# The score layout of the last segment and the order of the second half, in a fused attention and Fourier kernel

## The chip, the cores and the metric

The kernel runs on one core of a Trainium2 chip. The metric is device time in microseconds (us) of one execution. The engines work side by side, each through its own queue: TensorE (PE, with its weight loads shown apart as PEld), VectorE (DVE), ScalarE (ACT), GpSimd (POOL), and SyncE (SP), which issues most of the transfers. Before the change the median of three runs is 238.96 us (237.57 to 241.05).

## The reference, cut to what matters

There are 2048 tokens of 640 columns, 32 heads of 20 columns, and four segments of 512 tokens. Each segment has causal softmax attention of its own; beside it stands a linear-attention memory that gathers the segments already past.

```python
for s in range(N):                                  # N = 4 segments, L = 512
    logits = einsum('bhqd,bhkd->bhqk', qs, ks) * scale + mask
    a_dot = einsum('bhqk,bhkd->bhqd', softmax(logits), vs)
    a_mem = (phi(qs) @ M) / (phi(qs) @ z + 1e-06)
    outs.append(g * a_mem + (1.0 - g) * a_dot)
    M, z = M + phi(ks)^T vs, z + sum(phi(ks))
a = stack(outs) @ wo
b = irfft2(rfft2(B_x) * (w_r + 1j * w_i))           # Fourier filter, 2048 x 640
return gate * a + (1 - gate) * b                    # gate = sigmoid(x . gate_w)
```

The kernel takes A_x for the Fourier branch too.

## The kernel before, in words

Everything is one program of 2329 operations (an operation is one instruction, or for TensorE a group of matmuls). They are recorded with their dependencies (lines 866 to 889) and then put into the engines' queues in an order that is written out by hand: the list of numbers ORDER (line 639). Number v is operation v // 2, and v % 2 chooses between two engines where an operation has two, as most evictions of PSUM have (line 573: ACT or DVE) and many additions in SBUF (line 588: DVE or POOL). The method schedule (line 117) walks through the list, assigns PSUM banks and semaphores, and emits waits only where an operation depends on one of another engine. An engine works strictly through its own queue.

The work: projections of q, k, v and the gate for a segment, scores and exponentials, value products, memory update and memory read, and between these, to fill TensorE, the Fourier branch (matmuls named F1, D, T, Tb, Db; its result lies in the tile G). At the end the output projection (oproj) and the inverse transform's last step (Fb) of a 128-token tile accumulate in the same PSUM bank, and the tile is stored.

Scores. Heads are worked on in eight groups of four, and groups in four pairs. A unit of scores (qk_unit, line 1326) fills the four PSUM banks of the pool "qk" with matmuls of 20-row, 64-column tiles; ACT then takes the exponential of them into the tile ex; POOL zeroes what causality forbids (mask, line 1400, an affine_select over four heads at a time). As no other banks belong to that pool, a unit can begin only when the exponential of the unit before has read it. There are three kinds: "a" and "b" of 512 columns for one head group, and "c", the small pieces, 128 columns a group. Segments 1 and 2 are "wide" (line 1253): one c unit serves four groups and one ACT instruction of 128x2048 reads it. Segments 0 and 3 take a c unit for two groups (UNITS, line 633).

Segments 0 to 2 multiply values against the exponentials (pv_flipped, line 1256) and leave their results through the staging tiles ub and a store to DRAM. Segment 3 is different: pv_group (line 1409) uses the exponentials as the stationary operand (128 x 128) and the values as 21 moving columns; DVE divides by the denominator (pv_den, pv_rec, pv_mul), the memory's part is added (addmem), and the result is transposed on TensorE (oT3), projected, and stored last. Its exponentials have a layout of their own in ex, of 1280 columns a head: the b unit is written by two ACT instructions (320 and 192 columns of each of the four heads), a c unit by two (one for each group), lines 1349 to 1360. Because that layout overlaps the one of segment 2, the first three groups wait until certain groups of segment 2 are used up (ex3, line 1309).

Line 1407 marks a mask that starts at partition 64; schedule then makes POOL wait for the end of the instruction before, and the next POOL instruction for the end of this one (lines 211 and 212).

Of the kernel before, what the change touches and what calls it, by code (L numbers as in the profile page):

```python
# [12 lines left out]
P = 128  # L13
S = 2048
D = 640
# [495 lines left out]
class Kern:  # L511
# [84 lines left out]
    def dma(self, dst, src, nbytes, r, w, prio, tr=False, name="", after=(), queue="sp"):  # L596
# [656 lines left out]
    def wide(self, s):  # L1253
        return s in (1, 2)
# [47 lines left out]
    def exb(self, s, g, k):  # L1302
        if s == 3:
            return self.b("ex3", g % 3, k)
# [423 lines left out]
```

## Time and profile before

| what | value |
|---|---|
| median of three runs | 238.96 us |
| the profiled execution | 239.47 us |
| its span, first to last instruction | 237.7 us |
| its mean granted TensorE clock | 0.99 |
| TensorE busy | 224.2 us |
| VectorE, ScalarE, GpSimd busy | 194.9, 193.4, 150.7 us |
| exponentials of segment 3 | 166.1 to 224.1 us, 32 instructions, 36.2 us busy |

The profile lists busy time by engine, by stretch of time, and by line, operation and shape; "idle before <- X" is what an engine's idle time before an instruction was ended by. All matmuls bear line 567 or 565, the lines of the helper that emits them, so one tells them apart by the tiles that they read: qkp (scores), ex and va (values), big and Cp (Db), G (Fb), oU and oTl (projection). "issue" is time in which an engine waits for nothing that the profile shows. Beside the busy shares stands the granted clock of TensorE, 1.00 being full speed.

### The profile page before, as it was taken

The page shows a single profiled execution, that of the slowest core. Times are in us where ns is not written, and L with a number is a line of the kernel's source. Part 1 is how long each engine was busy: PE and PEld are TensorE (multiplying, and loading weights), DVE is VectorE, ACT ScalarE, POOL GpSimd, SP SyncE. Part 2 cuts the span into 40 slices and gives each one's busy share as a digit, 9 for nine tenths or more (in the row PEclk, how much of TensorE's full clock was granted, in tenths as well). Part 3 has the DMA queues.
Part 4 walks back from the last instruction along what each step waited for, and adds up shares of the span by engine and source line. Part 5 has one row for each costly group of instructions (what it writes and reads, how often), then busy time and mean ns, then how long its engine had stood idle before and what let it go on. Part 6 is the DMA issues. An engine that isn't in the chain of part 4 may idle for free.

```text
span 237.7 us, 10391 instructions
## 1 busy us (share of the span) xinstructions
PE 224.2 (94%) x4392; PEld 141.7 (60%) x4406; DVE 194.9 (82%) x497; ACT 193.4 (81%) x221; POOL 150.7 (63%) x299
## 2 busy tenths in 40 slices
PE   6899999999999999999999999899999799999992
PEld 2585677776555765555566456555454456567792
DVE  0499988899999978899999979998999748536662
ACT  2199889898999999999998989999997878487710
POOL 9223156466669777576867476679988494676810
PEclk9999999999999999999999999999999999799998
DMA  7999959999796659987537781786879498662124
GB/s 149 292 317 253 269 153 207 246 177 225 191 209 103 163 152 204 219 206 167 168 101 241 192 253 36 237 268 196 98 213 296 130 132 106 114 103 85 43 76 115
DMA packets 59268, 42.20 MB, mean 178 GB/s; under 512 B 30229, under 2 KB 55381, under 8 KB 59221
## 3 DMA queue, kind: packets, MB, share of 16 engines
q1 hardware_dynamic: 58180, 40.96, 73.5%
q8 instruction: 35, 0.57, 1.0%
q10 hardware_dynamic: 1040, 0.57, 0.9%
q14 instruction: 13, 0.10, 0.1%
HBM read 23.32 MB, written 12.30 MB: 150 GB/s over the span
## 4 chain that ended last, share of the span: by engine, by line
PE 66%; DVE 13%; DMA 10%; ACT 7%; issue 2%; SPq 1%; DVEq 0%
PE psum L567 59%; PE psum L565 7%; ACT ex L1367 4%; DVE Pt L1560 3%; DMA u_scr<-ub 2%; DMA pkn<-phk 2%; DMA Wt<-in_B_w_r_dram 2%; DMA xT<-in_A_x_dram 2%; DVE G L1606 1%; DMA dnc<-u_scr 1%; DVE va L1183 1%; ACT et L1140 1%; DVE ub L579 1%; DVE Cp L579 1%; DVE mem L1225 1%
## 5 line engine op out<-in xcount | busy, mean ns | idle before, releaser
L1404 POOL TENSOR_SCALAR_AFFINE_SELECT ex<-ex 128x256 bf16<-128x256 bf16 (+3 forms) x224 | 104.4, 485 | 43.2 <-ACT ex L1367 7.8
L1367 ACT ACTIVATE ex<-psum 128x2048 bf16<-128x2048 f32 (+1 forms) x56 | 101.7, 1816 | 7.4 <-PE psum L567 5.6
L1358 ACT ACTIVATE ex<-psum 128x1280 bf16<-128x1280 f32 (+3 forms) x32 | 36.2, 1130 | 10.6 <-PE psum L567 10.0
L567 PE MATMUL psum<-qkp 20*64 20x64 bf16 (+5 forms) x1280 | 32.2, 271 | 1.0 <-ACT ex L1367 0.8
L567 PE MATMUL psum<-xT,wk 128*128 128x256 bf16 (+1 forms) x280 | 32.2, 273 | 0.2
L567 PE MATMUL psum<-xT,wq 128*128 128x512 bf16 (+1 forms) x121 | 28.0, 380 | 2.6 <-DMA xT<-in_A_x_dram 1.8
L567 PE MATMUL psum<-wv,xT 128*32 128x321 bf16 (+3 forms) x385 | 26.8, 301 | 0.0
L1560 DVE TENSOR_TENSOR Pt<-psum,Wt 128x642 bf16<-128x642 f32 x32 | 25.5, 821 | 0.4
L567 PEld LDWEIGHTS psum<-xT,wk 128*128 128x128 bf16 (+1 forms) x280 | 20.1, 97 | 6.7 <-issue 1.5
L567 PEld LDWEIGHTS psum<-qkp 20*64 20x64 bf16 x1280 | 13.6, 103 | 17.2 <-ACT ex L1367 9.3
L565 PE MATMUL psum<-wo,oU 128*32 128x320 bf16 x480 | 21.8, 309 | 0.0
L973 POOL TENSOR_TENSOR xsb<-xf 128x320 bf16<-128x320 bf16 (+2 forms) x11 | 8.1, 744 | 19.4 <-DVE xf L968 10.5
L567 PE MATMUL psum<-big,Cp 128*128 128x321 bf16 (+1 forms) x96 | 19.4, 304 | 0.8 <-DVE eo L579 0.4
L579 DVE CAST ot<-psum 128x320 bf16<-128x320 f32 x21 | 9.9, 489 | 12.1 <-PE psum L565 9.7
L567 PE MATMUL psum<-big,Ac 128*128 128x160 bf16 (+2 forms) x96 | 18.2, 258 | 0.3 <-DVE va L1183 0.2
L567 PEld LDWEIGHTS psum<-wv,xT 128*32 128x32 bf16 (+1 forms) x385 | 13.4, 96 | 7.0 <-issue 1.8
L567 PE MATMUL psum<-ex,va 128*32 128x64 bf16 (+3 forms) x576 | 17.2, 256 | 0.3 <-ACT qu L577 0.3
L1183 DVE TENSOR_TENSOR va<-psum,ebx 128x320 bf16<-128x320 f32 x32 | 15.3, 484 | 1.9 <-PE psum L567 0.7
L567 PE MATMUL psum<-tt,Yt 128*128 128x256 bf16 (+1 forms) x96 | 16.1, 275 | 0.4 <-ACT qu L577 0.2
L1606 DVE TENSOR_TENSOR G<-eo,psum 128x320 bf16<-128x320 f32 x32 | 14.7, 479 | 2.1 <-PE psum L567 1.9
L567 PEld LDWEIGHTS psum<-ex,va 128*32 128x32 bf16 x576 | 10.9, 96 | 8.6 <-issue 1.3
L1140 ACT ACTIVATE et<-qu 128x512 bf16<-128x512 bf16 x25 | 15.6, 626 | 0.0
(101 smaller groups left out, 404.5 us busy)
## 6 DMA issues: line engine op xcount, KB each, us to landing
qkp<-qk_scr SPq DMA_DIRECT2D x28, 160.0 KB
tt<-tab_tt SPq DMA_DIRECT2D x8, 512.0 KB, 4.4
qk_scr<-qu SPq DMA_DIRECT2D x12, 256.0 KB, 3.8
u_scr<-ub SPq DMA_DIRECT2D x12, 256.0 KB, 5.6
xsb<-in_A_x_dram SPq DMA_DIRECT2D x8, 320.0 KB, 5.8
oU<-u_scr SPq DMA_DIRECT2D x15, 128.0 KB, 4.7
out_dram<-ot SPq DMA_DIRECT2D x12, 160.0 KB
Wt<-in_B_w_r_dram SPq DMA_DIRECT2D x16, 80.2 KB, 3.1
```

Source lines behind the costliest of these rows:

```text
L565: h = e.matmul(dst, wt, r_, start=st, stop=sp_, **{**kw, "tile_position": (0, q), "skip_group_check": True})
L567: h = e.matmul(o_, l_, r_, start=st, stop=sp_, **kw)
L579: alts["dve"] = (lambda e: e.tensor_copy(dst(), src()), 67 + 1.04 * n, 68.0)
L973: self.either(lambda e, dst=dst, src=src, d0=d0, n=n, op=op: e.tensor_tensor(xs.ap(o + dst, [D, 2], [1, n]), xf.ap(src + d0, [321, 2], [1, ...
L1140: self.one("act", lambda e: e.activation(et.ap(0, [1, L]), qsl(), ACT.Exp), L, [qb], [b("et", pi_)], late, fix=95, name="phi_exp")
L1183: self.one("dve", lambda e: e.tensor_tensor(va.ap(i * H * VW + h0 * VW, [VW, nh], [1, DH]), self.ps(bank, 0, [DH, nh], [1, DH]), self.ebx. ...
L1225: fn = lambda e: e.tensor_tensor(self.mem.ap(i * D + 64 * q, [4, 16], [P, 5], [1, 4]), self.ps(bank, 0, [VW, 16], [4, 5], [1, 4]), dn.ap(1 ...
L1358: self.one("act", lambda e, d=d, q=q: e.activation(self.ex.ap(*d), self.ps(bank, *q), ACT.Exp, scale=SC), (2048, (1280, 768)[x], 512)[kind ...
L1367: self.one("act", lambda e, d=d, q=q: e.activation(self.ex.ap(*d), self.ps(bank, *q), ACT.Exp, scale=SC), 2048 if kind < 2 else 512 * n, [ ...
L1404: self.one("pool", lambda e: e.affine_select(self.ex.ap(*d, p0=p0, np_=np_), self.ex.ap(*q, p0=p0, np_=np_), [[0, 4], [1, n]], ALU.is_ge, ...
L1560: self.one("dve", lambda e, ri=ri, Pt=Pt, Wt=Wt, wo_=wo_, bank=bank: e.tensor_tensor(Pt.ap(ri * 322, [644, 2], [1, KD]), self.ps(bank, 0, ...
L1606: self.one("dve", lambda e, q=q, n2=n2, bank=bank, eo=eo: e.tensor_tensor(self.G.ap(n2 * D + 639 * q, [1 - 2 * q, 320]), eo.ap(q, [1, 320] ...
```

## The change

Segment 3 takes the layout of segments 1 and 2: a pitch of 1088 columns a head, one full-width exponential for a b unit, and one c unit for four groups. Where its small pieces of groups 4 to 7 and the masked copies for the third block of queries land, other tiles are used up by then: the staging tiles ub (and what follows them) and the accumulator Macc of the memory; the operations wait for those. The value products read their stationary blocks from the new places. Masks of segment 3: two for each a, two for each b and three for the small pieces of each group, as before; one of the three now starts at partition 64. The wait ex3 is gone.

ORDER is written anew from the first quarter on, with the numbers shifted where operations fell away (2313 for 2329). TensorE's queue is the same up to its 215th operation, which starts at 44.8 us, and has only small swaps up to about 92 us. 46 operations that both kernels have change their engine. In the new list the value products of groups 1, 2 and 3 follow one another on TensorE, with three matmuls of Db ahead of them and among them the score unit a of group 4 alone; before, groups 2, 3 and 1 stood between score units and projections.

```diff
-        self.ex = T("ex", [P, self.ONCOL + 4 * D])
+        self.ex = T("ex", [P, self.X2COL + 3 * 4 * P])
...
-    def wide(self, s):
-        return s in (1, 2)
+    def wide(self, s, pr):
+        return s > 0
...
+    UBCOL = ONCOL + 2 * 4 * D
+    X2COL = UBCOL + 4 * L + 4 * P
...
     def exo(self, s, g):
-        return g % 3 * 5120 if s == 3 else self.EBASE + ((s * 8 + g) % 3) * 4 * self.EPITCH
+        return self.EBASE + ((s * 8 + g) % 3) * 4 * self.EPITCH

     def exc(self, s, g):
-        return 512 * g if g < 4 else self.MBASE + 768 + 512 * (g - 4)
+        return 512 * g if g < 4 else (self.UBCOL if s == 3 else self.MBASE + 768) + 512 * (g - 4)
...
-            if kind == 0:
-                outs = [((e0, [1280, 4], [1, 512]), (0, [512, 4], [1, 512]))]
-            elif kind == 1:
-                outs = [((e0 + 576, [1280, 4], [1, 320]), (0, [512, 4], [1, 320])), ((e0 + 960, [1280, 4], [1, 192]), (320, [512, 4], [1, 192]))]
-            else:
-                outs = [((e0 + 896 + x * step, [1280, 4], [320, 2], [1, 64]), (x * 128, [512, 4], [64, 2], [1, 64])) for x in range(2)]
...
+        if kind == 2:
+            d, q = (self.exc(s, g), [128, 4], [512, n], [1, 128]), (0, [512, 4], [128, n], [1, 128])
         else:
-            if kind == 2:
-                d, q = (self.exc(s, g), [128, 4], [512, n], [1, 128]), (0, [512, 4], [128, n], [1, 128])
...
+            d, q = (e0 + 576 * kind, [self.EPITCH, 4], [1, 512]), (0, [512, 4], [1, 512])
...
+        if s == 3 and kind == 2 and pr > 1:
+            home = [b("ub", k, x) for k in range(2) for x in range(2)]
...
+            else:
+                self.mask(s, g, P, (x0 + 64, cp), (e0 + 896, ep), 64, ("b0",), ("x2",), prio, 64)
+        elif s == 3:
+            self.mask(s, g, P, (x0, cp), (c0, cp), 64, ("c0",), ("x2c",), prio, 0)
+            self.mask(s, g, 64, (c0, cp), None, 64, (), ("c0",), prio, 0, 64)
+            self.mask(s, g, 64, (c0, cp), None, P, (), ("c0",), prio, -64)
...
+                 after=[self.b("Macc", t) for t in range(5)] * (wk[0][0] == "x"))
...
+            o = e0 + hh * self.EPITCH
+            if jj < 2:
+                return self.ex.ap(o + jj * 512 + (i - jj) * P, [1, P])
+            return self.ex.ap(c0 + hh * P if jj == 3 else x0 + hh * P if i == 2 else o + 960, [1, P])
```

More of the change, by code (lines that the diff above doesn't have):

```diff
@@ L822, in alloc @@
         self.Macc = T("Macc", [P, 880], F32)
+        assert self.ub[0].off == self.ex.off + 2 * self.UBCOL and self.Macc.off == self.ex.off + 2 * self.X2COL
         self.Mz = [T(f"Mz{i}", [P, 880]) for i in range(2)]
@@ L1235, in attend @@
         for pr in range(4):
-            if self.wide(s):
+            if self.wide(s, pr):
                 units = (((0, 1, 2, 3), 2),) * (pr % 2 == 0) + (((0,), 0), ((0,), 1), ((1,), 0), ((1,), 1))
@@ L1300 @@
     ONCOL = MBASE + 512
+    UBCOL = ONCOL + 2 * 4 * D
+    X2COL = UBCOL + 4 * L + 4 * P
     def exb(self, s, g, k):
-        if s == 3:
-            return self.b("ex3", g % 3, k)
+        if s == 3 and (k[0] == "x" or k == "c0" and g > 3):
+            return self.b("ex3", g % 3 if k[0] == "x" else g, k)
         if k == "c0":
@@ L1307, in exb @@
         return self.b("ex", (s * 8 + g) % 3, k)
-    def ex3(self, g):
-        b = self.b
-        e = lambda x: [b("ex", x, k) for k in ("a0", "b0", "m1")]
-        return ([b("exc", x) for x in range(4)] + e(0), e(0) + e(1), e(1) + e(2) + [b("ex", x, "m3") for x in range(3)])[g]
     def exo(self, s, g):
-        return g % 3 * 5120 if s == 3 else self.EBASE + ((s * 8 + g) % 3) * 4 * self.EPITCH
+        return self.EBASE + ((s * 8 + g) % 3) * 4 * self.EPITCH
     def exc(self, s, g):
-        return 512 * g if g < 4 else self.MBASE + 768 + 512 * (g - 4)
+        return 512 * g if g < 4 else (self.UBCOL if s == 3 else self.MBASE + 768) + 512 * (g - 4)
     def exm(self, s, g):
@@ L1323, in exall @@
     def exall(self, s, g):
-        return [self.exb(s, g, k) for k in ("a0", "b0", "c0", "m1", "m3") + ("b1",) * (s == 3)]
+        return [self.exb(s, g, k) for k in ("a0", "b0", "c0", "m1") + (("m3",) if s < 3 else ("x2", "x2c"))]
     def qk_unit(self, s, pr, u, unit):
@@ L1348, in qk_unit @@
         e0, n = self.exo(s, g), len(gps)
-        if s == 3:
-            step = self.exo(s, g + 1) - e0 if kind == 2 else 0
-            if kind == 0:
-                outs = [((e0, [1280, 4], [1, 512]), (0, [512, 4], [1, 512]))]
-            elif kind == 1:
-                outs = [((e0 + 576, [1280, 4], [1, 320]), (0, [512, 4], [1, 320])), ((e0 + 960, [1280, 4], [1, 192]), (320, [512, 4], [1, 192]))]
-            else:
-                outs = [((e0 + 896 + x * step, [1280, 4], [320, 2], [1, 64]), (x * 128, [512, 4], [64, 2], [1, 64])) for x in range(2)]
-            for x, (d, q) in enumerate(outs):
-                self.one("act", lambda e, d=d, q=q: e.activation(self.ex.ap(*d), self.ps(bank, *q), ACT.Exp, scale=SC), (2048, (1280, 768)[x], 512)[kind], [bank],
-                         [self.exb(s, 2 * pr + (x if kind == 2 else gp), ks + str(x * (kind == 1))) for gp in gps], prio - self.QK_LEAD, name="exp" + str(x)[x == 0:],
-                         after=[q for gp in gps if 2 * pr + gp < 3 for q in self.ex3(2 * pr + gp)])
-        else:
-            if kind == 2:
-                d, q = (self.exc(s, g), [128, 4], [512, n], [1, 128]), (0, [512, 4], [128, n], [1, 128])
-            else:
-                d, q = (e0 + 576 * kind, [self.EPITCH, 4], [1, 512]), (0, [512, 4], [1, 512])
-            home = [b("xf", k) for k in range(3)] if s == 0 and kind == 2 and pr > 1 else []
-            self.one("act", lambda e, d=d, q=q: e.activation(self.ex.ap(*d), self.ps(bank, *q), ACT.Exp, scale=SC), 2048 if kind < 2 else 512 * n, [bank],
-                     [self.exb(s, 2 * pr + gp, ks + "0") for gp in gps], prio - self.QK_LEAD, name="exp", after=home)
@@ new lines, in qk_unit @@
+        if kind == 2:
+            d, q = (self.exc(s, g), [128, 4], [512, n], [1, 128]), (0, [512, 4], [128, n], [1, 128])
+        else:
+            d, q = (e0 + 576 * kind, [self.EPITCH, 4], [1, 512]), (0, [512, 4], [1, 512])
+        home = [b("xf", k) for k in range(3)] if s == 0 and kind == 2 and pr > 1 else []
+        if s == 3 and kind == 2 and pr > 1:
+            home = [b("ub", k, x) for k in range(2) for x in range(2)]
+        self.one("act", lambda e, d=d, q=q: e.activation(self.ex.ap(*d), self.ps(bank, *q), ACT.Exp, scale=SC), 2048 if kind < 2 else 512 * n, [bank],
+                 [self.exb(s, 2 * pr + gp, ks + "0") for gp in gps], prio - self.QK_LEAD, name="exp", after=home)
@@ L1375, in masks @@
         e0, c0, m0 = self.exo(s, g), self.exc(s, g), self.exm(s, g)
-        ep = [1280 if s == 3 else self.EPITCH, 4]
+        ep = [self.EPITCH, 4]
         cp = [P, 4]
-        if s < 3:
-            if ks == "a":
-                self.mask(s, g, P, (e0 + 512, ep), (e0, ep), 64, ("a0",), ("m1",), prio, 64)
-                self.mask(s, g, P, (e0, ep), None, P, (), ("a0",), prio, 0)
-            elif ks == "b":
-                self.mask(s, g, 64, (e0 + 512, ep), None, P, (), ("b0", "m1"), prio, -64)
-                self.mask(s, g, P, (e0 + 896, ep), None, 64, (), ("b0",), prio, 64)
-            else:
-                self.mask(s, g, 64, (m0, [64, 4]), (c0, cp), 64, ("c0",), ("m3",), prio, 0, 64)
-                self.mask(s, g, P, (c0, cp), None, 64, (), ("c0",), prio, 0)
-                self.mask(s, g, 64, (c0 + 64, cp), None, 64, (), ("c0",), prio, 0)
-        elif ks == "a":
+        x0 = self.X2COL + g % 3 * 4 * P
+        if ks == "a":
             self.mask(s, g, P, (e0 + 512, ep), (e0, ep), 64, ("a0",), ("m1",), prio, 64)
@@ L1393, in masks @@
             self.mask(s, g, 64, (e0 + 512, ep), None, P, (), ("b0", "m1"), prio, -64)
-            self.mask(s, g, P, (e0 + 960, ep), None, 64, (), ("b1",), prio, 64)
-        else:
-            self.mask(s, g, P, (e0 + 1152, ep), (e0 + 896, ep), 64, ("c0",), ("m3",), prio, 64)
-            self.mask(s, g, P, (e0 + 896, ep), None, 64, (), ("c0",), prio, 0)
-            self.mask(s, g, 64, (e0 + 1152, ep), None, P, (), ("c0", "m3"), prio, -64)
+            if s < 3:
+                self.mask(s, g, P, (e0 + 896, ep), None, 64, (), ("b0",), prio, 64)
+            else:
[4 more added lines that the diff above has]
+            self.mask(s, g, 64, (c0, cp), None, P, (), ("c0",), prio, -64)
+        else:
+            self.mask(s, g, 64, (m0, [64, 4]), (c0, cp), 64, ("c0",), ("m3",), prio, 0, 64)
+            self.mask(s, g, P, (c0, cp), None, 64, (), ("c0",), prio, 0)
+            self.mask(s, g, 64, (c0 + 64, cp), None, 64, (), ("c0",), prio, 0)
     def mask(self, s, g, np_, d, q, n, rk, wk, prio, base, p0=0):
@@ L1405, in mask @@
             self.ex.ap(*d, p0=p0, np_=np_), self.ex.ap(*q, p0=p0, np_=np_), [[0, 4], [1, n]], ALU.is_ge, 0.0, base=base, channel_multiplier=-1), 4 * n,
-            [self.exb(s, g, k) for k in rk], [self.exb(s, g, k) for k in wk], prio, per=0.793, fix=218, name="mask")
+            [self.exb(s, g, k) for k in rk], [self.exb(s, g, k) for k in wk], prio, per=0.793, fix=218, name="mask",
+                 after=[self.b("Macc", t) for t in range(5)] * (wk[0][0] == "x"))
         self.Sc.ops[-1].part = p0 > 0
@@ L1415, in pv_group @@
         e0 = self.exo(s, g)
+        c0, x0 = self.exc(s, g), self.X2COL + g % 3 * 4 * P
         def weights(hh, i, jj):
-            o = e0 + hh * 1280
-            if jj == 0:
-                return self.ex.ap(o + i * P, [1, P])
-            if jj == 1:
-                return self.ex.ap(o + 512 + (i - 1) * P, [1, P])
-            return self.ex.ap(o + 896 + (i - 2) * P if jj == 2 else o + 1152, [1, P])
+            o = e0 + hh * self.EPITCH
+            if jj < 2:
+                return self.ex.ap(o + jj * 512 + (i - jj) * P, [1, P])
+            return self.ex.ap(c0 + hh * P if jj == 3 else x0 + hh * P if i == 2 else o + 960, [1, P])
         if True:
@@ L1435, in pv_group @@
                         items.append((th, 22))
-                self.mms(items, [self.exb(s, g, k) for k in (("a0",), ("a0", "b0", "m1"), ("a0", "b0", "b1", "c0", "m1"), ("a0", "b0", "b1", "c0", "m1", "m3"))[i]] + [b("va", s % 2, jj) for jj in range(i + 1)] + [bank], [],
+                self.mms(items, [self.exb(s, g, k) for k in (("a0",), ("a0", "b0", "m1"), ("a0", "b0", "m1", "x2", "x2c"), ("a0", "b0", "c0", "m1"))[i]] + [b("va", s % 2, jj) for jj in range(i + 1)] + [bank], [],
                          prio, name="pv")
```

128 rows, old and new, of the table ORDER are left out of this document.

## The prediction, made before the result

> **What bounds the kernel now.** I read the page first, then busy time by stage, then the chain of waits, and last the instructions of the last segment.
>
> ```profile
> span 237.7 us, 10391 instructions
> PE 224.2 (94%) x4392; PEld 141.7 (60%) x4406; DVE 194.9 (82%) x497; ACT 193.4 (81%) x221; POOL 150.7 (63%) x299
> ...
> PEclk9999999999999999999999999999999999799998
> ```
>
> TensorE (PE) has work for 224.2 of 237.7 us; no other engine comes near. Only 13.5 us of the span are idle on it, and that is all that a change which leaves its matmuls alone can win. One slice before the end has a lower granted clock. By stage (window; busy of PE, PEld, DVE, ACT, POOL; clock; DMA):
>
> ```profile
> 170.00:180.00 10.00, 9.59 (x166) 4.92 (x165) 9.65 (x29) 9.41 (x12) 8.67 (x15) 1.00 0.78 216
> 180.00:190.00 10.00, 8.92 (x198) 4.90 (x195) 8.49 (x22) 7.64 (x9) 5.60 (x13) 1.00 0.63 193
> 190.00:200.00 10.00, 9.76 (x250) 6.39 (x250) 6.09 (x16) 7.74 (x10) 7.31 (x16) 1.00 0.95 125
> 200.00:210.00 10.00, 9.29 (x247) 5.68 (x247) 5.48 (x17) 6.53 (x10) 6.15 (x11) 0.83 0.70 103
> 210.00:220.00 10.00, 10.00 (x332) 7.20 (x324) 6.04 (x15) 7.92 (x7) 7.94 (x15) 1.00 0.32 95
> 220.00:230.00 10.00, 10.00 (x308) 8.23 (x300) 5.86 (x17) 4.76 (x7) 5.91 (x12) 1.00 0.21 64
> ```
>
> Until 180 us PE, VectorE (DVE) and ScalarE (ACT) are all nearly full, so a wait of one soon becomes a wait of another. From 180 us on, the stage of the last segment's scores, ACT and DVE have room and PE is the limit. The chain of waits says the same (start, length, what):
>
> ```profile
> 178.57 5.58 DMA u_scr<-ub
> ...
> 190.23 0.98 PE psum L567 x8
> ...
> 223.48 9.52 PE psum L567 x276
> 233.00 0.02 issue
> 233.02 0.90 DVE ot L579 x2
> ```
>
> From 190.23 us the chain stays on PE to 233.00, then an eviction and a store end it. Who waited for whom between 155 us and the end (total, times, longest):
>
> ```profile
> ACT ex L1358 <- PE psum L567: 10.0, 12, 2.3
> ...
> PEld psum L567 <- issue: 5.5, 19, 0.8
> ...
> PEld psum L567 <- ACT ex L1358: 2.2, 8, 0.3
> ```
>
> The exponentials of the last segment (line 1358) wait 10.0 us for PE; PE's weight loads wait 2.2 us for them. The half that the change makes cheaper is the half that waits.
>
> **The change part by part.** First the exponentials. Their rows between 160 and 226 us, by shape (busy, mean ns), and two of their places on ACT:
>
> ```profile
> L1358 ACT ACTIVATE ex<-psum 128x2048 bf16<-128x2048 f32 x8 | 15.0, 1877 | 5.4 <-PE psum L567 5.3
> L1358 ACT ACTIVATE ex<-psum 128x1280 bf16<-128x1280 f32 x8 | 9.9, 1236 | 2.1 <-PE psum L567 2.0
> ...
> L1358 ACT ACTIVATE ex<-psum 128x768 bf16<-128x768 f32 x8 | 6.5, 810 | 0.3
> L1358 ACT ACTIVATE ex<-psum 128x512 bf16<-128x512 f32 x8 | 4.8, 597 | 2.9 <-PE psum L567 2.7
> ```
>
> ```profile
> 186.32 2.08 ACT L1358 ACTIVATE ex<-psum 128x1280 bf16<-128x1280 f32 x2
> 189.21 0.44 ACT L577 ACTIVATE eo<-psum 128x321 f32<-128x321 f32 x1 [0.80 <-PE psum L567]
> 189.69 1.23 ACT L1358 ACTIVATE ex<-psum 128x512 bf16<-128x512 f32 x2
> ```
>
> Before, a "b" unit is a pair of 2.08 us and a "c" unit of two head groups a pair of 1.23. After, each b unit is one full-width instruction (1.877), and four groups of c share one (1.877 again). ACT saves 8 x (2.08 - 1.88) = 1.6 us and 4 x 1.23 - 2 x 1.88 = 1.16 us, together 2.8 us, in 18 instructions for 32. On the path I take 0, because ACT idles 10.0 us in front of these instructions for PE. Without that cover it would be at most the 2.2 us for which PE's loads wait on them. The low end is 0, since no row shows ACT behind.
>
> The matmuls: each head group's score pieces and all 320 value products stay as they are, so PE's work is unchanged, 0. But a unit is also a change of matmul form (20x64 tiles for scores, 128x128, 128x32), and each such change leaves the weight loader idle (in brackets, us):
>
> ```profile
> 206.70 0.16 PEld L567 LDWEIGHTS psum<-qkp 20*64 20x64 bf16 x12 [0.26 <-issue]
> 207.06 0.12 PEld L565 LDWEIGHTS psum<-wo,oU 128*32 128x32 bf16 x8 [0.20 <-POOL ex L1404]
> ...
> 209.21 0.15 PEld L567 LDWEIGHTS psum<-qkp 20*64 20x64 bf16 x12 [0.27 <-ACT ex L1358]
> 209.56 0.10 PEld L567 LDWEIGHTS psum<-G,fbg 128*32 128x32 bf16 x4 [0.20 <-ACT ot L577]
> ```
>
> Score units fall from 20 to 18. Reading PE's order out of the number lists, I count 213 changes of form before and 207 after. Six fewer at 0.20 to 0.27 are 1.2 to 1.6 us on the engine that sets the end; the low end is 0, if the drain of the matmuls ahead covers the idle loader. I take 1.2, the smaller row.
>
> The masks: still 56 in this segment. Eight of 128x256 become 64x256 that start at partition 64, and line 1407 makes GpSimd (POOL) finish the instruction before and this one before the next. Two plain ones back to back against three of that kind, in an earlier segment:
>
> ```profile
> 130.03 0.78 POOL L1404 TENSOR_SCALAR_AFFINE_SELECT ex<-ex 128x256 bf16<-128x256 bf16 x2 [0.68 <-DVE phq L1153]
> ...
> 143.06 1.36 POOL L1404 TENSOR_SCALAR_AFFINE_SELECT ex<-ex 64x256 bf16<-64x256 bf16 x3 [0.40 <-DVE Yt L1565]
> ```
>
> 0.39 each against 0.45, and the two borders inside the second row serve three instructions, so about 0.1 us a border. Eight masks have 16 borders at most: 1.6 us more on POOL. I take 0 on the path: POOL is 55 to 79% busy from 180 to 220 us, and between 160 and 226 us one engine waited once for a mask:
>
> ```profile
> who waited for it (us, times):
>   PEld psum L565: 0.2, 1
> ```
>
> Without that cover it costs up to 1.6. Waiting behind a late mask would be the value product at the head of PE's queue, and with it every matmul behind it, then ACT.
>
> New waits: the c exponential of groups 4 to 7 now lands in the memory of the staging buffers "ub" and waits for their last store, which the chain above shows landing at 178.57 + 5.58 = 184.15 us. It heads the third of the four pairs of head groups, beside work that now runs near 200 us, so 0; up to 1.9 (one such exponential late) if it came early. The new masks into the accumulator's memory wait for updates that ended a segment earlier: 0. Gone is the wait of the first three groups for the old layout's memory; no row of ACT above shows it, since PE ended those waits: 0.
>
> Moves: 46 instructions change engine, most of them evictions. ACT has 214 for 229 in its queue (18 for 32 exponentials, one eviction less), DVE 501 for 497, POOL 292 for 295. An eviction is 0.44 on ACT by the row above and not much more on DVE, so no engine shifts by over 2 us over 140 us: 0 on the path, 0.5 either way in the full stage before 180 us. SyncE's queue holds the same 239 transfers, ACT's the same eight stores at the end, in partly another order; POOL issues none. Their moves are by a few places and I cost them at nothing, under PE's work; the bound is a wait of the size that PE shows for such things, 0.7.
>
> The stall: here is what lowered the clock (PE in order of time; then busy by stretches, with the clock after POOL):
>
> ```profile
> 201.26 0.27 PE L567 MATMUL psum<-va,ex 128*128 128x21 bf16 x5
> 202.25 0.46 PE L567 MATMUL psum<-va,ex 128*128 128x21 bf16 x11 [0.71 <-issue]
> ```
>
> ```profile
> 201.00:202.00 1.00, 0.54 (x13) 0.35 (x9) 1.00 (x4) 0.97 (x2) 0.34 (x1) 1.00 0.45 84
> 202.00:203.00 1.00, 0.75 (x16) 0.48 (x20) 0.53 (x3) 0.59 (x1) 0.23 (x1) 0.69 0.26 95
> 203.00:204.00 1.00, 1.00 (x20) 0.52 (x20) 1.00 (x4) 0.00 (x0) 1.00 (x1) 0.50 0.49 153
> 204.00:205.00 1.00, 1.00 (x40) 0.46 (x36) 0.34 (x1) 0.11 (x1) 1.00 (x3) 0.50 1.77 164
> 205.00:206.00 1.00, 1.00 (x24) 0.65 (x20) 0.00 (x0) 0.97 (x2) 1.00 (x2) 0.60 0.71 147
> ```
>
> In the middle of one group's value products (21 columns each) PE stood 0.71 us for nothing that the profile shows, and right after it the clock was about half for over 3 us: (1 - 0.69) + 0.5 + 0.5 + 0.4 = 1.7 us of clock lost. Hole and clock together are 2.4 us. After, groups 1, 2 and 3 come as one stretch of 120 value products with one score unit and three other matmuls between, denser than before; so the place where this happened stays. I take 0; ends: 2.4 won, or another 1.7 lost.
>
> [...]
>
> Sum, against the profiled execution: 239.47 us, its span 237.7 and 1.8 around it. 239.47 - 1.2 (forms) - 0 = 238.3. That execution lies 0.5 above the median 238.96, so for a median 237.8.
>
> **The rivals.** (1) *Nothing moves*: the loader's idle time at a change of form is covered, as a PE of 10.00 in 10.00 us from 210 us on would allow. 239.0. Against it: PE's busy time is modelled, and the loader does stand still. (2) *The hole and the half clock go*, since both hang on where instructions fall: 237.8 - 2.4 = 235.4, with the 2.2 us of waits for exponentials on top at most 233.2. For it: a hole of "issue" is no dependency of the program; against it: the stretch is denser, and 19 such waits (5.5 us) say that they arise anywhere. (3) *Slower: POOL falls behind.* Its 1.6 us make the masks late for the dense stretch; group 3's last mask now stands on POOL behind masks of groups 1, 2 and 3 of both kinds, and its value products stand at the head of PE's queue. 1.6 of hole and 1.7 of half clock: 237.8 + 3.3 = 241.1. It decides from the point where the masks end after PE reaches that group. Against it: the single 0.2 us wait above.
>
> **How the numbers follow.** Forecast 0.42, nothing moves 0.18, second rival 0.18, POOL late 0.22. The likeliest is 237.8, its own range 236.9 (forms 0.4 more, evictions 0.5) to 239.5 (forms 1.2 less, evictions 0.5). For 8 in 10 the range reaches to the second rival's lower end, 233.2, and past the third to 242.3 (0.5 for evictions, 0.7 for transfers). A measurement of this kernel can tell about 2% from no change, 4.8 us. Below 234.2 lies only the far end of the second rival: 0.12. Above 243.7 there would have to be a late POOL and a second half clock: 0.10. Within 2%: 0.78.
>
> **What would show it.** Right: the b and c units of the last segment are 18 exponentials of about 1.88 us each, ACT idles more than 10 us before them, PE is still 94% or more, and the chain stays on PE from about 190 us. The forms are right if PE's end comes 1 to 2 us earlier with the same holes. Rival 2 shows as a clock row without a low digit before the tail; rival 3 as weight loads waiting for masks by over 1 us. The prediction is wrong if the full stage before 180 us gains a wait on DVE, or if the order makes PE wait for transfers.

## The result and the profile after

The changed kernel takes 240.5 us (median of 20 runs, 237.9 to 244.41) against 238.74 us for the kernel before (20 runs, 237.28 to 242.22). The ratio is 1.0071, 95% interval [1.0044, 1.0099]: slower by 0.7%, some 1.7 us, which is under the 2% that the prediction set as its bound, and to the other side of its forecast. (Medians here and below are over all runs; ratios, and counts called "in the ratio", leave out runs of a kernel over 1.5% above its fastest.) The profiled execution took 240.39 us. One matmul (fcat, xsb), in the part of TensorE's queue that both kernels share, starts at 28.31 us in it and at 26.63 us in the profile of before; so 1.7 us lie between the two profiles that the change did not make, and their spans can't be compared as they are. From its page:

```profile
span 238.6 us, 10375 instructions
...
PE 227.3 (95%) x4391; PEld 142.0 (60%) x4406; DVE 195.7 (82%) x501; ACT 190.8 (80%) x206; POOL 148.5 (62%) x296
...
PEclk9999999999999999999999999999999998599999
...
q8 instruction: 34, 0.56, 1.0%
```

ACT has become cheaper by 2.6 us (193.4 to 190.8), and TensorE (PE) is busy for 3.1 us more although it runs the same matmuls. The clock row has an 8 and a 5 side by side, one slice earlier than the single 7 of before. Busy time by stage (stretch of time; busy of PE, PEld, DVE, ACT, POOL; clock; DMA):

```profile
190.00:200.00 10.00, 10.00 (x324) 7.62 (x321) 7.54 (x20) 7.83 (x7) 6.95 (x14) 1.00 0.58 149
200.00:210.00 10.00, 9.12 (x174) 4.74 (x174) 5.99 (x20) 4.20 (x4) 4.90 (x9) 0.66 0.29 71
210.00:220.00 10.00, 10.00 (x304) 6.99 (x296) 4.88 (x11) 8.39 (x7) 7.46 (x14) 1.00 0.43 96
220.00:230.00 10.00, 10.00 (x310) 7.96 (x306) 7.22 (x23) 4.93 (x5) 5.24 (x11) 1.00 0.23 70
```

Between 190 and 200 us PE gets 324 matmuls done where before it did 250: most products of groups 1 to 3 are here. In the next 10 us it gets 174 done instead of 247, at a mean clock of 0.66 instead of 0.83. PE in order of time across that border:

```profile
195.80 1.26 PE L565 MATMUL psum<-wo,oU 128*32 128x320 bf16 x32
...
197.93 2.61 PE L567 MATMUL psum<-va,ex 128*128 128x21 bf16 x98
201.42 0.34 PE L567 MATMUL psum<-va,ex 128*128 128x21 bf16 x6 [0.89 <-issue]
201.69 0.65 PE L567 MATMUL psum<-qkp 20*64 20x512 bf16 x12
202.28 0.60 PE L567 MATMUL psum<-va,ex 128*128 128x21 bf16 x16
202.72 1.23 PE L567 MATMUL psum<-big,Cp 128*128 128x321 bf16 x4
```

The hole of "issue" is still there (0.89 us for 0.71), again within the value products of group 1. The clock events of the trace, which the following rows resolve to a microsecond, have half speed from 201.34 to 208.17 us: 6.83 us, twice 3.41. Before, it was once 3.41 (202.38 to 205.79). In what follows, a stretch of 3.41 us is called a window.

```profile
201.00:202.00 1.00, 0.58 (x18) 0.44 (x18) 1.00 (x6) 0.00 (x0) 0.78 (x2) 0.67 0.17 22
202.00:203.00 1.00, 1.00 (x26) 0.61 (x19) 0.32 (x1) 0.09 (x1) 0.76 (x1) 0.50 0.32 102
...
207.00:208.00 1.00, 1.00 (x20) 0.64 (x16) 0.00 (x0) 1.00 (x1) 0.93 (x3) 0.50 0.03 8
208.00:209.00 1.00, 1.00 (x36) 0.66 (x27) 0.49 (x2) 0.03 (x1) 0.16 (x1) 0.92 0.74 156
```

Who waited for whom between 155 us and the end (total, times, longest), and the chain of waits at the place:

```profile
ACT ex L1354 <- PE psum L567: 12.4, 17, 2.9
...
PEld psum L567 <- issue: 5.1, 16, 1.0
...
PEld psum L567 <- ACT ex L1354: 2.9, 11, 0.3
```

```profile
197.06 3.48 PE psum L567 x134
200.54 0.89 issue
201.42 4.65 PE psum L567 x51
...
225.34 8.98 PE psum L567 x255
```

Nothing else took PE's place. The exponentials (now line 1354) wait for PE even longer than before, 12.4 us for 10.0, and no wait of PE for a mask (line 1388) over 0.3 us stands in this list. The 51 matmuls after the hole need 4.65 us.

How often does it happen? A mean clock of 0.987 or less over a run is about two windows at half speed (0.013 x 238 = 3.1 us; 6.83 us at half give 3.4). The mean does not say where they lie: the profile of before_cols22 has slow products near 80 us too (two of 512 columns at 80.56 us took 0.98 us; in before, at 76.54 us, two took 0.59). Of the 20 runs of after, 15 are that low, 9 of the 14 in the ratio. Of 98 runs of the kernel before, taken beside the experiments below, 16 are, but none of the 65 in the ratio; 60 have 0.9945 or more, less than one such window. So the profiled run of before, with its 0.99, was not the usual one; that of after is. Within the runs of after, those at 0.987 or less and in the ratio have a median of 240.4 us, and the three at 0.997 or more took 237.9, 238.17 and 238.99. The half clock costs about 2.2 us. Without it the three stand where the 60 runs of before do, whose median is 238.16.

### The profile page after: what moved, and what is told of

It reads as the page before. It is cut to its first block, busy times and chain, and to the rows that moved or that the text cites. A ratio compares the mean times of both kernels' runs of the same rounds, so it can differ in the third digit from the quotient of the medians.

```text
span 238.6 us, 10375 instructions
## 1 busy us (share of the span) xinstructions
PE 227.3 (95%) x4391; PEld 142.0 (60%) x4406; DVE 195.7 (82%) x501; ACT 190.8 (80%) x206; POOL 148.5 (62%) x296
## 4 chain that ended last, share of the span: by engine, by line
PE 68%; ACT 12%; DMA 9%; DVE 6%; issue 2%; SPq 1%; POOL 0%
PE psum L567 60%; ACT ex L1354 8%; PE psum L565 8%; DMA qkp<-qk_scr 3%; DMA oU<-u_scr 2%; DMA pkn<-phk 2%; DMA xT<-in_A_x_dram 2%; ACT et L1141 2%; SPq L600 1%; DVE Bt L579 1%; ACT qu L577 1%; DVE Pt L1545 1%; ACT Cp L577 1%; DVE va L1184 1%; SPq L602 1%
## 5 line engine op out<-in xcount | busy, mean ns | idle before, releaser
L1354 ACT ACTIVATE ex<-psum 128x2048 bf16<-128x2048 f32 (+1 forms) x74 | 135.5, 1830 | 18.8 <-PE psum L567 17.2
L567 PE MATMUL psum<-xT,wk 128*128 128x256 bf16 (+1 forms) x280 | 33.5, 286 | 0.2
L567 PEld LDWEIGHTS psum<-qkp 20*64 20x64 bf16 x1280 | 13.7, 103 | 16.5 <-ACT ex L1354 10.9
L567 PE MATMUL psum<-big,Ac 128*128 128x160 bf16 (+2 forms) x96 | 17.3, 257 | 0.3 <-DVE va L1184 0.2
L567 PE MATMUL psum<-tt,Yt 128*128 128x256 bf16 (+1 forms) x96 | 16.8, 275 | 0.6 <-DVE va L1184 0.2
L565 PEld LDWEIGHTS psum<-wo,oU 128*32 128x32 bf16 x480 | 12.8, 100 | 5.5 <-issue 1.6
```

The source lines that it names most:

```text
L565: h = e.matmul(dst, wt, r_, start=st, stop=sp_, **{**kw, "tile_position": (0, q), "skip_group_check": True})
L567: h = e.matmul(o_, l_, r_, start=st, stop=sp_, **kw)
L1354: self.one("act", lambda e, d=d, q=q: e.activation(self.ex.ap(*d), self.ps(bank, *q), ACT.Exp, scale=SC), 2048 if kind < 2 else 512 * n, [ ...
```

## The experiments

Theory 1: the hole in the instruction stream lets the clock fall, and its place in the dense stretch makes it worse. Theory A: the stretch itself does it, because its products have few moving columns (21 each), although PE never idles. Rival B: the new layout or the new waits cost the time, and the clock is a companion. (The expectations of the first four runs call theory A rival A.) All were measured against the kernel before on the same chip.

**1 and 2. Shifting PE's instructions (after_shift64, before_shift64).** The holes lie at nearly the same place of PE's own list, its 7012th load or matmul before and its 7020th after. The page's row "q8 instruction" has 34 packets of some 16.5 KB; if all are PE's, that is one for some 260 of its 8800 loads and matmuls. From this the author took as an estimate that instructions come in blocks and that one begins there. Sixty-four small matmuls at the start would then move the edge by 128 instructions.

```diff
             self.mms([(lambda k=k: (self.ps(bank, 0, [1, L]), ...), 1000)],
+                     + [(lambda: (self.ps(bank, 0, [1, 16]), t.ap(0, [1, P]), t.ap(P, [1, 16]), True, True, {}), 16)] * (64 * (k == 9)),
```

> The changed kernel with 64 matmuls of 16 columns added to its warm-up, so that every later instruction of PE stands 128 places further on in its instruction stream; nothing else differs. Theory 1 (the hole in the value products is PE's instruction stream running dry at the edge of a fetched block of 256 instructions, and the hole lets the clock fall): the edge now falls 128 instructions earlier in the program, where the block before it is eaten more slowly; the hole of 0.9 us is gone or under 0.3, at most one half-clock window is left, and the time falls from 240.5 by 1.7 to 4.3 us, to 236.2 to 238.8 (up to 1 us more if the added matmuls delay the start). Rival A (the dense stretch of 21-column products halves the clock by itself): the half-clock windows stay, 239.6 or more. Rival B (layout or order cost time elsewhere): 240.5.

> The kernel before with the same 64 added matmuls. Theory 1: its hole of 0.7 us at the same place of the stream and the half-clock window go too; 238.7 falls by up to 2.4, to 236.3 to 237.5 (up to 1 us more from the added matmuls). Rival A: its value products are not as dense, so nothing changes, 238.7. Rival B says nothing here: 238.7.

After, shifted: 240.71 us (6 runs), ratio 1.0121 [1.0065, 1.0176]. Before, shifted: 240.95 us (12 runs), ratio 1.0084 [1.0041, 1.0128]; neither fell as theory 1 expected. Why both are slower stays open: in the trace of after_shift64 the added matmuls delay the first projection by only 0.18 us (7.35 for 7.17) and the stretch by 0.25. So these ratios say little, and the trace says more. PE in order of time in after_shift64, then its stages:

```profile
198.18 2.86 PE L567 MATMUL psum<-va,ex 128*128 128x21 bf16 x104
200.97 0.43 PE L567 MATMUL psum<-qkp 20*64 20x512 bf16 x12
201.33 0.58 PE L567 MATMUL psum<-va,ex 128*128 128x21 bf16 x16
201.76 1.23 PE L567 MATMUL psum<-big,Cp 128*128 128x321 bf16 x4
```

```profile
190.00:200.00 10.00, 10.00 (x315) 7.55 (x312) 7.77 (x19) 8.08 (x7) 7.15 (x15) 1.00 0.67 145
200.00:210.00 10.00, 10.00 (x200) 5.58 (x200) 6.25 (x20) 4.70 (x5) 5.64 (x9) 0.66 0.51 89
```

The hole is gone, PE is busy for 20.00 of 20.00 us, and the clock falls to the same 0.66. Theory 1 fell in this run: the hole isn't needed. But only 2 of the 6 runs are at 0.987 or less, against 15 of 20 with the hole; six runs can't settle whether the hole makes the fall more frequent. The one profile of before_shift64 is of a run of 246.66 us, where the fastest took 239.12, so its time can't be compared. In it the value products run without a hole; PE stands for 3.74 us behind its 7268th load or matmul (206.34 to 210.08 us), 256 behind the 7012th, which fits blocks of 256, and a lower clock follows there (0.96 from 200 to 210 us, 0.70 from 210 to 220).

**3. The layout with the old order (layout_alone).** The operations of after in the order of before; three masks are put behind the ones that they depend on.

```diff
-ORDER: the list of after
+ORDER: the list of before, renumbered; on POOL mask b0.1, b1.1, b6.1 directly behind b0.0, b1.0, b6.0
```

> The new score layout with the old order: each queue as before, the c units of four groups where the first of two stood, the dropped instructions left out, and three masks moved behind the ones that they now depend on. Theory 1: the stretch of value products is not denser than before, so one half-clock window as before, and the saved forms show: 237.5 to 239. Rival B with the layout as the cause (POOL's masks from partition 64, the waits for ub): 240 or more. If the old order does not fit the new layout and the moved masks come late: 240 to 243, with PE's loads waiting for masks.

It took 244.11 us (6 runs), ratio 1.0258 [1.0192, 1.0324], 5 of 6 runs at 0.987 or less. So theory 1's forecast of 237.5 to 239 missed here too, and the time is above the 240 to 243 that were expected of late masks. PE:

```profile
197.14 0.59 PE L565 MATMUL psum<-wo,oU 128*32 128x320 bf16 x12
199.66 0.28 PE L567 MATMUL psum<-va,ex 128*128 128x21 bf16 x4 [1.94 <-POOL ex L1381]
200.25 0.39 PE L567 MATMUL psum<-va,ex 128*128 128x21 bf16 x8 [0.30 <-POOL ex L1381]
```

In the old order the masks (line 1381 here) come 2.2 us late: group 3 stands before group 1 there, and its masks follow a c unit that now serves four groups. The layout does not fit the old order, so this run can't price the layout by itself. It shows that the prediction's third rival, late masks, is a real mechanism of this layout, which the order of after avoids. Here the clock falls (0.96 from 190 to 200 us, 0.69 from 200 to 210) behind a stretch in which PE waits (8.00 of 10 us busy) rather than one that is dense.

**4. The dense stretch taken apart (after_spread).** Six operations of the tail go between the value products; "final#3" on DVE goes back behind the sums.

```diff
-pv1.0 pv2.0 pv2.1 pv1.1 pv2.2 pv2.3 pv3.0 pv3.1 pv3.2 pv3.3 pv1.2 qk_a4 pv1.3
+pv1.0 pv2.0 pv2.1 pv1.1 pv2.2 pv2.3 Fb#3 oproj#15..19 pv3.0 pv3.1 pv3.2 pv3.3 pv1.2 qk_a4 pv1.3
```

> The changed kernel with one bank's six projection operations (Fb and five oproj of the tile's second half) moved from ahead of the second c unit into the stretch, between the value products of groups 2 and 3, and the eviction of that bank moved two places back on DVE. Theory 1: the block is eaten about as fast (projections take 17 ns an instruction, value products 14), so the hole stays at 0.5 to 1.0 us and the time changes by less than 0.7 either way. Rival A (density alone): the clock stays full or falls for one window alone, 1.7 us faster, 238.8 or less. Two more changes of form cost 0.2 to 0.5 under both.

242.96 us (6 runs), ratio 1.0136 [1.0043, 1.0228], 4 of 6 at 0.987 or less. One break of 1 us, with the hole left in (0.70 us within pv1.2), wasn't enough in its profile, which is of the run of 248.57 us, at a mean clock of 0.965, and has slow products near 80 us besides (four of 154 columns at 80.04 us took 0.70 us; at 72.33 us four took 0.43). Whether the move cost time of its own isn't shown. It decides nothing.

**5 to 7. More columns, same instructions (after_cols48, before_cols48, after_cols32).** The value products read and write 48 or 32 columns instead of 21. Instructions, order and waits stay; the extra columns are overwritten or not read.

```diff
-    return (self.ps(bank, i * 88 + hh * VW, [1, DH + 1]),
+    n = min(48, (H - 4 * g - hh) * VW)
+    return (self.ps(bank, i * 88 + hh * VW, [1, n]),
             weights(hh, i, jj),
-            va.ap(jj * H * VW + (4 * g + hh) * VW, [1, DH + 1]), jj == 0, jj == i, {})
+            va.ap(jj * H * VW + (4 * g + hh) * VW, [1, n]), jj == 0, jj == i, {"skip_group_check": True})
```

> The changed kernel with 48 moving columns in each value product in place of 21 (fewer where fewer values follow): the same instructions in the same order with the same waits, the extra results fall on places that the next head's product writes over. [...] 240.5 falls by 2.4 to 3.4, to 237.1 to 238.1, and the mean clock is 0.996 or more in nearly all runs. Theory 1 (the hole itself lowers the clock): hole and half clock stay, 240 or more. Rival B (layout or order cost time elsewhere): 240.5.

> The kernel before with 48 columns in its value products in the same way. Theory A: few of its executions have a half-clock window ahead of the end, since its value products stand apart, so the median changes little, by 0 to 1.0 us down, 237.4 to 238.4; the hole stays. Together with the changed kernel of the same width it gives what layout and order are worth without the clock: under theory A with the saved changes of form, the changed one is 0 to 1.2 us faster; if layout or order lose elsewhere, slower.

> The changed kernel with 32 columns in its value products. [...] So half-clock windows in some of the runs, fewer than with 21 columns: median between the other two, 238 to 240. Theory 1: as with 21 columns, 240.5.

| kernel | median us (runs) | ratio to before | runs at clock 0.987 or less | of these in the ratio |
|---|---|---|---|---|
| after, 21 columns | 240.5 (20) | 1.0071 [1.0044, 1.0099] | 15 of 20 | 9 of 14 |
| after_cols32 | 239.74 (12) | 1.0027 [0.9976, 1.0078] | 6 of 12 | 1 of 7 |
| after_cols48 | 238.59 (12) | 1.004 [1.0003, 1.0078] | 2 of 12 | 1 of 10 |
| before_cols48 | 239.18 (12) | 1.0076 [1.0038, 1.0114] | 0 of 12 | 0 of 12 |

This is the test that tells theory A from theory 1 and rival B: nothing is changed but the number of columns that a product moves, more work in fact, and the half clock goes away by degrees: 15 of 20 runs with 21 columns, 6 of 12 with 32, 2 of 12 with 48. The ratio of after_cols32 leaves out five of its six runs with a low clock and so says little of them. The time of after_cols48, 238.59, missed the 237.1 to 238.1 expected for theory A; that of after_cols32, 239.74, lies in the 238 to 240 expected for it. Why 48 columns make the kernel before slower stays open; its clock is full.

**8 and 9. The stretch put into the kernel before (before_gather), and a control (before_cols22).** Without any part of the new layout, PE's queue of before is brought to the shape of after. The control asks for 22 columns, with the same edit as above.

```diff
-Db#93 pv2.0 pv2.1 Db#94 Db#95 pv2.2 pv2.3 qk_a5 Db#84 oproj#17..19 pv3.0 pv3.1 Db#85 Db#86 pv3.2 pv3.3 qk_b6 pv1.0 pv1.1 pv1.2 Db#87 Db#88 pv1.3 Db#89
+Db#93 Db#94 Db#95 pv2.0 pv2.1 pv2.2 pv2.3 pv1.0 pv1.1 pv1.2 pv1.3 qk_a5 pv3.0 pv3.1 pv3.2 pv3.3 oproj#17..19 Db#84 Db#85 Db#86 qk_b6 Db#87 Db#88 Db#89
```

> The kernel before with its value products of groups 2, 1 and 3 brought together on PE as in the changed one: 120 products with the one score unit a5 between, the three Db and three projection operations that stood between them moved behind. [...] If the density is not the cause: the clock stays at 0.995 in most runs, 238.5 to 239.5 (a score unit waits up to 0.8 us longer for its exponential).

> A control: the kernel before with 22 columns in each value product in place of 21, everything else the same, so that no theory gives it another time than the kernel before (238.5). If it comes out slower by about 0.7%, as the one with 48 columns did, then a mere rebuild of this kernel costs that much, and differences below 1% between two kernels prove little; if it comes out the same within 0.4%, the 48 columns themselves cost 1.8 us in the kernel before.

before_gather: 241.24 us (12 runs) beside 239.72 (29 runs), ratio 1.0103 [1.0061, 1.0146]; 10 of 12 runs at 0.987 or less (6 of the 8 in the ratio), beside 8 of 29 (none of the 18 in the ratio). Control: 238.27 us, ratio 0.9963 [0.991, 1.0016], 1 of 12. PE of before_gather, then its stage:

```profile
195.73 2.43 PE L567 MATMUL psum<-va,ex 128*128 128x21 bf16 x80
198.09 0.43 PE L567 MATMUL psum<-qkp 20*64 20x512 bf16 x12
198.45 0.46 PE L567 MATMUL psum<-va,ex 128*128 128x21 bf16 x12
199.43 0.86 PE L567 MATMUL psum<-va,ex 128*128 128x21 bf16 x28 [0.51 <-POOL ex L1397]
```

```profile
200.00:210.00 10.00, 9.47 (x194) 4.80 (x194) 6.72 (x17) 6.12 (x8) 5.34 (x8) 0.66 0.30 74
```

The old layout with the dense stretch has the same 0.66 and loses about as much as the change did; 241.24 lies above the 238.5 to 239.5 that were expected if the density is not the cause. Rival B isn't needed. The run isn't a clean stretch: PE waits 0.51 us for a mask in it, and 0.53 us for an eviction behind it, and what these waits cost beside the clock isn't separated.

**10 to 12. More columns in the dense stretch alone (after_cols48_mid, after_cols40_mid, before_cols40_mid).** The edit is shown against after_cols48; the other two have 40 in place of 48.

```diff
-    n = min(48, (H - 4 * g - hh) * VW)
+    n = 48 if 0 < g < 4 else DH + 1
```

> The changed kernel with 48 columns in the value products of groups 1, 2 and 3 alone, the dense stretch; the others keep 21. Theory A: the half-clock windows go as with 48 columns everywhere, mean clock 0.995 or more in most runs, 238.0 to 238.8. If the wide products of the other groups were what helped: 240 or more.

> The kernel after, with 40 moving columns instead of 21 in the value products of groups 1, 2 and 3 alone; the extra columns are overwritten or not read. If the half clock goes by how much the array is given to do in a window, 40 columns lie above 32 (half clock in 6 of 12 runs) and near 48 (in 0 of 12): at most 2 of 12 runs with a mean clock of 0.987 or less. If nothing but 48 columns cures it, 4 or more of 12. Against the same edit in the kernel before, run beside it: 1.2 us faster if the fewer changes of matmul form are worth what the prediction said; equal within 0.5 us if they are covered; slower if the new order costs something besides the clock.

> The kernel before with the same 40 columns in groups 1, 2 and 3. The kernel before halves its clock there in few runs, so by the clock theory the edit wins under 0.5 us: within 0.5 us of the kernel before. It is the yardstick for the run beside it: both have the half clock taken away, and the rest of the change is what lies between them. If 48 columns in all groups were slower than before (1.0076) because of the added columns in the quiet tail, which these three groups do not touch, this one is not slower.

after_cols48_mid: 239.0 us (12 runs) beside 239.72 (29), ratio 0.9994 [0.9943, 1.0045], 0 of 12 at 0.987 or less. after_cols40_mid: 238.22 us (12 runs) beside 238.72 (23), ratio 1.0015 [0.9974, 1.0055], 2 of 12. before_cols40_mid: 239.36 us (12 runs), ratio 1.0022 [0.9977, 1.0067], which keeps 5 of its 12 runs, 3 of 12. The page, PE in order of time and a stage of after_cols48_mid:

```profile
PEclk9999999999999999999999999999999999999999
```

```profile
196.94 2.62 PE L567 MATMUL psum<-va,ex 128*128 128x48 bf16 x98
200.16 0.32 PE L567 MATMUL psum<-va,ex 128*128 128x48 bf16 x6 [0.60 <-issue]
200.41 0.43 PE L567 MATMUL psum<-qkp 20*64 20x512 bf16 x12
200.77 0.57 PE L567 MATMUL psum<-va,ex 128*128 128x48 bf16 x16
201.19 0.71 PE L567 MATMUL psum<-big,Cp 128*128 128x321 bf16 x4
```

```profile
200.00:210.00 10.00, 9.43 (x252) 5.95 (x256) 6.51 (x19) 7.15 (x6) 7.22 (x12) 1.00 0.60 100
```

Here 98 products of 48 columns take 2.62 us, those of 21 columns took 2.61. The hole stands where it stood (0.60 us), the clock stays at 1.00, the four matmuls after it take 0.71 us for 1.23, and 252 matmuls get done in these 10 us for 174. From the first of the 98 products to the end of the span this kernel needs 235.1 - 196.94 = 38.2 us and after 238.6 - 197.93 = 40.7: 2.5 less, 0.3 of it in the hole, so 2.2 for the clock, the same as between the runs of after. The ratios agree: 0.9994 / 1.0071 is 0.8% less, with the two intervals combined 0.6%. It gives the loss back. That it beats the kernel before isn't shown.

## Why the prediction was wrong, point by point

- **What bounds the kernel: right.** PE is busy for 95%, the chain stays on it to the end, ACT waits for it.
- **Exponentials, 0 on the path and 2.8 us off it: right.** ACT's busy time fell by 2.6 us, and its waits for PE rose from 10.0 to 12.4.
- **Masks, new waits, moves, 0: not contradicted** in the order of after: no wait of PE for a mask over 0.3 us stands in its list. (The wait behind a mask that starts at partition 64 is put into the program in lines 259 and 260; lines 211 and 212, named above, estimate it.) The third rival didn't come; layout_alone shows what it was worth (2.2 us of hole) where the order doesn't fit the layout.
- **Fewer changes of matmul form, 1.2 us won: not seen, and not ruled out.** With the half clock made rarer in both, after_cols40_mid against before_cols40_mid is 1.0015 / 1.0022 = 0.999, and with the two intervals combined about 0.6%, so -0.2 us give or take 1.4; after_cols48 against before_cols48 is 1.004 / 1.0076 = 0.996, so -0.9 us give or take 1.3. The loader's waits on "issue" and on the exponentials together are 5.1 + 2.9 = 8.0 us after and 5.5 + 2.2 = 7.7 before: there are fewer units, but no less waiting. The traces have the 213 and 207 changes that were counted, but from the 2600th of the 4406 weight loads on (some 155 us) there are 76 before and 74 after: four of the six fewer ones lie in the stage where other engines are nearly full too.
- **The failed step is "The stall", in the words "so the place where this happened stays. I take 0".** The prediction named the end, "another 1.7 lost", and the reason, a stretch denser than before, and then gave it no weight. It failed in two ways. It took the profiled half clock for a part of every run, so that keeping it would be worth nothing; but 60 of 98 runs of before have less than one such window. And the dense stretch doesn't keep what was there: 15 of 20 runs have the clock of two windows. Measured, the term is +2.2 us in a run that has it; over the runs in the ratio that is (9 / 14 - 0 / 65) x 2.2 = 1.4 of the 1.7 us found, an estimate from the mean clocks, which lies within the interval of what was found, 1.0 to 2.4. Two rows hinted at it beforehand: the clock row against the median, 0.5 us below the profiled run, and the low digit right behind value products.
- **Why two windows: not shown.** In the 3.41 us ahead of half speed PE was busy for 2.61 us with 100 matmuls in after, and for 2.71 us with 88 in before. In the first 3.41 us at half speed after got 47 matmuls done and in the next 57, before got 76; full speed followed the 57 and the 76. That little work behind the stretch keeps the clock low is the author's guess.
- **What went with the fall.** The time that PE is busy does not tell it: half speed came with PE busy for 20.00 of 20.00 us (after_shift64). A wait does not either: the slow products of before_cols22 near 80 us stand behind waits of 0.64 and 1.83 us for a transfer, while in before_cols48, behind waits of 0.79 and 1.81 us for it, two products of 512 columns took 0.59 us, as in before. In the dense stretch the products of 21 columns moved 0.79 columns a ns in after (98 in 2.61 us), 0.76 in after_shift64 (104 in 2.86) and 0.69 in before_gather (80 in 2.43), and half speed followed in each of these profiles; those of 48 columns moved 1.80 in after_cols48_mid (98 in 2.62), and the clock stayed at 1.00. For scale, 28 products of 256 columns at 13.45 us in after moved 2.2 (3.23 us). How few columns it takes isn't shown; that more columns in otherwise equal instructions make the half clock rare is shown by the clocks of the runs in the table.

## What to carry to other kernels

Bringing products with few moving columns together cost nothing in instruction time here (27 ns each), but for 2.6 us they moved 0.8 columns a ns, where products of 256 columns moved 2.2, and 15 of 20 runs had the clock of two windows at half speed. Spread such products among wide matmuls, as in the kernel before (that clock in 16 of 98 runs), or give them columns that nobody reads (in 2 of 12 with 48). Look for the dip in the clock row right after the light stretch, not in it: here the stretch ran from 197.93 us and half speed from 201.34. Before a term is taken from one profiled run, set its clock and its time against the other runs: a dip that is in at most 38 of 98 runs can't be kept or won like an instruction.

## What the runs showed of the hardware that was not expected

- A value product takes 2.61 us / 98 = 27 ns with 21 columns and 27 ns with 48 (2.62 / 98), so from 21 to 48 columns the number of columns does not set the pace.
- The clock fell with PE busy for 20.00 of 20.00 us (after_shift64, 0.66 from 200 to 210 us). Half speed lasted 6.83 us in after and 3.41 us in before.
- The page has 34 instruction packets of 16.5 KB. A hole for nothing that the profile shows, of 0.89 us in after, 0.60 in after_cols48_mid and 0.70 in after_spread, stood behind the same value product, the 98th of the stretch, and left it when 128 instructions were put ahead (after_shift64: 104 in 2.86 us without a hole). That a late fetch makes it isn't shown: in after the last packet ahead of the hole ended at 199.97 us, 0.57 us before the hole began, and the next began at 202.52, 1.1 us after its end.
